# GpSimd multiplications that wait for a planned VectorE operation, three small copies on ScalarE, and a new order

## The chip, the cores and the metric

One core of a Trainium2 chip. Times are device microseconds of the whole program. The kernel before ran at a median of 355.24 us in three runs (353.91 to 357.82).

The program uses five engines of this core: TensorE (PE in the profile, its weight loads PEld), VectorE (DVE), ScalarE (ACT), GpSimd (POOL) and SyncE (SP, here an issuer of DMAs). The program gives each engine its instructions in a fixed order and ties the engines together with semaphores.

## The reference

```
q_p, k_p = phi(q), phi(k)              # phi(x): p = x @ w_phi ; p -= max|p| ; [exp(p), exp(-p)]
kv  = einsum('bhsf,bhsd->bhfd', k_p, v)
num = einsum('bhsf,bhfd->bhsd', q_p, kv)
den = einsum('bhsf,bhf->bhs', q_p, sum_s k_p) + 1e-6
x   = (num / den) as [batch, seq, heads*64]
x1, x2, x3 = split(x @ w_proj)         # 512 wide each
y   = x1 * irfft(rfft(x2) * rfft(filter)) * x3     # along seq, 576 long
out = y @ w_out
```

8 batches, 8 heads, 576 positions, 64 per head, 128 features. Inputs and output are fp32; the kernel works in bf16 with fp32 accumulation.

## The kernel before

The program is a list of 2467 nodes. A node is a few instructions of one engine; a fixed list ORDER gives the order in which nodes are emitted, and with it the order on each engine. A second list, SLOTS, gives each PSUM tile its bank. The work comes in 16 attention units (two per batch, nodes a0 to a15) and 8 batches of convolution and gate (m0 to m7).

Per unit, GpSimd does six multiplications: the values, scaled by exp(-max) or exp(max), for the key-value matmuls.

```python
def f_v(hp, sg):                       # nodes v00 v01 v10 v11: 128x512
    def f():
        v12 = c.v12[pair(hp) % 3]
        nc.gpsimd.tensor_tensor(
            out=v12[:, sg, :, 0:HD].rearrange("p (j c) d -> p j c d", j=2),
            in0=c.vs[b % 2][:, g, hp:hp + 3:2],
            in1=v12[:, sg, :, 64:65].rearrange(
                "p (j c) o -> p j c o", j=2).to_broadcast([P, 2, 4, HD]),
            op=ALU.mult)
    return f
# ... f_vt: the same for the last 64 rows, 128x260
```

VectorE folds the transposed attention output twice (f1 to f4), and copies some of it:

```python
def level2(sl, op):                    # nodes f3 f4: two SBUF inputs
    def f():
        eo = get_eo()
        TT(out=get_G()[0][:, k0:k0 + 2, sl, 0:145], in0=eo[:, :, :, 0:145],
           in1=eo[:, :, :, 288:143:-1], op=op)
    return f

def rem():                             # node fr, "the rest copy"
    G, Gr = get_G()
    nc.vector.tensor_copy(Gr[:, k0:k0 + 2, :, 0:17], G[:, k0:k0 + 2, :, 128:145])

def f_x0():                            # node x0, "the edge copies", before f1 and f2
    nc.vector.tensor_copy(xT()[:, kt0 + 1, 512:SEQ], xT()[:, kt0 + 1, SEQ:640])
    nc.vector.tensor_copy(xT()[:, kt0:kt0 + 2, SEQ:SEQ + 1],
                          xT()[:, kt0:kt0 + 2, 0:1])

def f_mx0():                           # node mx0: 128x20, fp32 to bf16, "the cast"
    nc.vector.tensor_copy(c.M2[i2][:, 0:20], mxq().rearrange("p c h -> p (c h)"))

def f_mtc():                           # node mt, from PSUM, "the transposed maxima"
    nc.vector.tensor_copy(c.mT[i2], c.open[n + "mtp"])
# ... cut: maxima, exponentials, products with the filter's spectrum (L1026), Y (L1032) and so on
```

Nodes that use the SBUF port that VectorE and GpSimd share are marked `lock=1`. In the kernel before the mark has no effect on the program. It is emitted like this:

```python
with tc.manual_schedule(engines={ET.PE, ET.Activation, ET.DVE, ET.Pool, ET.SP}):
    for i in ORDER:
        if nodes[i].fn is not None:
            nodes[i].fn()
```

## Time and profile before

| | before |
|---|---|
| median time | 355.24 us |
| span of the profiled run | 352.1 us |
| VectorE busy | 317.5 us (90%) |
| TensorE busy | 306.6 us (87%) |
| ScalarE / GpSimd busy | 270.1 / 163.1 us |
| chain that ended last | TensorE 45%, VectorE 43% |

The page of the kernel before: its span, the busy table (microseconds, share of the span, instructions), and the chain of work that ended last, followed back from the last instruction.

```profile
span 352.1 us, 8527 instructions
...
PE 306.6 (87%) x3253; PEld 202.3 (57%) x3253; DVE 317.5 (90%) x742; ACT 270.1 (77%) x664; POOL 163.1 (46%) x207
...
PE 45%; DVE 43%; DMA 6%; ACT 2%; issue 2%; DVEq 0%; ACTq 0%
```

Two engines look full, and the chain alternates between them. But a busy engine may be waiting inside an instruction. The timeline shows that (kernel before, in order of time; columns: start, duration, engine, line, operation, output<-inputs, count; in brackets the idle time before it and what ended it).

```profile
211.92 0.45 DVE L333 TENSOR_TENSOR eo_118<-xT_115 128x578 bf16<-128x578 bf16 x1
...
212.75 1.05 POOL L759 TENSOR_TENSOR v_104<-vs_73,v_104 128x512 bf16<-128x512 bf16 x1 [10.62 <-ACT v_104 L750]
...
212.91 0.92 DVE L980 COPY xT_115<-xT_115 128x2 bf16<-128x2 bf16 x1
...
213.77 0.90 POOL L799 TENSOR_TENSOR vt_107<-vt_135,emt_84 128x260 bf16<-128x260 bf16 x1
...
214.12 2.11 DVE L333 TENSOR_TENSOR eo_119<-xT_115 128x578 bf16<-128x578 bf16 x2
...
214.63 1.27 POOL L759 TENSOR_TENSOR v_106<-vs_73,v_106 128x512 bf16<-128x512 bf16 x1
...
215.87 1.28 POOL L759 TENSOR_TENSOR v_104<-vs_73,v_104 128x512 bf16<-128x512 bf16 x1
...
216.15 1.69 DVE L340 TENSOR_TENSOR G_681<-eo_118 128x580 bf16<-128x580 bf16 x2
```

A fold alone takes 0.45 us (first line). Beside multiplications two of them take 2.11 us, and a copy of two elements takes 0.92 us. VectorE and GpSimd go forward in lockstep.

From the trace I worked out one number, the **collision loss**: for each VectorE instruction, the time from the end of the one before it (or its own start, if later) to its own end, less the median of its line and shape; losses over 0.1 us are summed. It is 36.7 us here, of which 30 lie where the chain runs through VectorE. The losses in the first 16 us of the program, which meet no GpSimd multiplication, are in it too.

I also asked, for each stalled operation that could be placed in ORDER, whether the multiplication that it met comes earlier or later in ORDER. In 33 of 34 cases it comes later. GpSimd, busy only 46% of the time, runs ahead of its place in the plan.

### The profile page before, as it was taken

How to read it: one execution, taken by the hardware profiler on the slowest of the kernel's cores; microseconds unless marked ns; L12 is line 12 of the kernel's file. 1: busy time of each engine (PE TensorE's matmuls, PEld its weight loads, DVE VectorE, ACT ScalarE, POOL GpSimd, SP SyncE). 2: the span in 40 equal slices, each digit the busy share in tenths (PEclk: the TensorE clock that was granted, in tenths of full speed). 3: DMA queues.
4: the chain of work that ended last, by engine and by line, in shares of the span. 5: the costliest groups of instructions: out<-in, count | busy, mean ns of one | idle time of the engine just before them, and what ended most of it. 6: DMA issues, size and time to landing. Idle time of an engine off the chain costs nothing.

```text
span 352.1 us, 8527 instructions
## 1 busy us (share of the span) xinstructions
PE 306.6 (87%) x3253; PEld 202.3 (57%) x3253; DVE 317.5 (90%) x742; ACT 270.1 (77%) x664; POOL 163.1 (46%) x207
## 2 busy tenths in 40 slices
PE   1478796799989699899989998889998999999984
PEld 0346653368547385468736774469556864586441
DVE  8999998989989989999988999999999999998390
ACT  1698785389969388698979997878888997994633
POOL 8859764509635802485038904670457214330000
PEclk9987998999999899999999999999999999999999
DMA  7999999918976927449671995292792461001013
GB/s 98 137 164 173 158 154 178 179 36 80 187 200 83 128 48 188 127 52 153 136 195 16 135 187 179 56 129 40 140 186 52 55 165 61 0 2 62 2 60 149
DMA packets 97160, 39.87 MB, mean 113 GB/s; under 512 B 66080, under 2 KB 92000, under 8 KB 97120
## 3 DMA queue, kind: packets, MB, share of 16 engines
q0 software_dynamic: 40096, 16.85, 39.9%
q1 hardware_dynamic: 57024, 22.49, 29.4%
q8 instruction: 25, 0.41, 0.5%
q14 instruction: 15, 0.12, 0.1%
HBM read 33.75 MB, written 9.44 MB: 123 GB/s over the span
## 4 chain that ended last, share of the span: by engine, by line
PE 45%; DVE 43%; DMA 6%; ACT 2%; issue 2%; DVEq 0%; ACTq 0%
DVE mxk_82 L736 3%; DMA xT_115<-xn_113 3%; DMA xT_114<-xn_113 3%; DVE xn_113 L917 3%; DVE mxq_147 L675 3%; DVE G_681 L340 3%; DVE mxq_143 L675 2%; DVE Y L1032 2%; DVE P_973 L1026 2%; DVE P_974 L1026 2%; DVE eo_119 L333 2%; DVE ts L1091 2%; DVE mxk_83 L736 1%; DVE G_684 L340 1%; DVE eo_118 L333 1%
## 5 line engine op out<-in xcount | busy, mean ns | idle before, releaser
L1067 PEld LDWEIGHTS <-wproj 128*128 128x128 bf16 x512 | 33.8, 99 | 36.2 <-issue 13.5
L759 POOL TENSOR_TENSOR v_105<-vs_73,v_105 128x512 bf16<-128x512 bf16 x12 | 13.3, 1116 | 35.3 <-ACT emt_84 L792 16.5
L759 POOL TENSOR_TENSOR v_106<-vs_73,v_106 128x512 bf16<-128x512 bf16 x10 | 11.1, 1114 | 26.1 <-ACT v_106 L750 18.9
L1161 PEld LDWEIGHTS <-yT 128*128 128x128 bf16 x144 | 13.8, 98 | 15.2 <-DVE yT L1132 2.2
L1026 DVE TENSOR_TENSOR P_973<-CS,H_124 128x1024 bf16<-128x1024 bf16 (+1 forms) x24 | 17.3, 720 | 5.6 <-ACT CS L1021 5.5
L759 POOL TENSOR_TENSOR v_106<-vs_72,v_106 128x512 bf16<-128x512 bf16 x10 | 11.4, 1153 | 19.9 <-PE fi_2944 L1161 12.0
L759 POOL TENSOR_TENSOR v_104<-vs_73,v_104 128x512 bf16<-128x512 bf16 x10 | 11.6, 1171 | 19.5 <-ACT v_104 L750 19.5
L851 PEld LDWEIGHTS <-sel 128*128 128x128 bf16 x256 | 18.6, 100 | 2.9 <-issue 0.3
L759 POOL TENSOR_TENSOR v_104<-vs_72,v_104 128x512 bf16<-128x512 bf16 x12 | 13.3, 1108 | 10.2 <-ACT v_104 L750 10.1
L759 POOL TENSOR_TENSOR v_105<-vs_72,v_105 128x512 bf16<-128x512 bf16 x10 | 10.9, 1086 | 13.7 <-ACT v_105 L750 13.7
L1026 DVE TENSOR_TENSOR P_974<-CS,H_125 128x1024 bf16<-128x1024 bf16 (+1 forms) x24 | 17.0, 719 | 0.0
L842 PEld LDWEIGHTS <-wpp 128*128 128x128 bf16 x128 | 11.3, 99 | 7.1 <-issue 2.8
L1115 PEld LDWEIGHTS <-Y 128*128 128x128 bf16 x128 | 12.5, 98 | 2.9
L799 POOL TENSOR_TENSOR vt_107<-vt_131,emt_84 128x260 bf16<-128x260 bf16 x8 | 5.2, 661 | 15.2 <-ACT emt_84 L792 15.2
L517 POOL DMA_DIRECT2D qt<-in_q_dram x18 | 11.6, 647 | 0.4 <-DMA kt<-in_k_dram 0.4
L517 POOL DMA_DIRECT2D kt<-in_k_dram x18 | 11.6, 647 | 0.0
L1010 PEld LDWEIGHTS <-G_681 128*128 128x128 bf16 x64 | 6.1, 98 | 9.0 <-DVE G_681 L340 1.7
L1010 PEld LDWEIGHTS <-G_684 128*128 128x128 bf16 x64 | 6.1, 98 | 8.9 <-issue 2.7
L525 POOL DMA_DIRECT2D vt_135<-in_v_dram x16 | 10.2, 635 | 0.0
L525 POOL DMA_DIRECT2D vt_131<-in_v_dram x16 | 10.0, 635 | 0.2 <-issue 0.2
L669 PEld LDWEIGHTS <-qT_76 128*128 128x128 bf16 x64 | 6.1, 104 | 6.2 <-DVE qT_76 L632 3.5
L500 POOL DMA_DIRECT2D ks<-in_k_dram x9 | 8.3, 923 | 2.0 <-PE ttp L640 1.2
(2109 smaller groups left out, 1366.9 us busy)
## 6 DMA issues: line engine op xcount, KB each, us to landing
ks<-in_k_dram POOLq DMA_DIRECT2D x7, 512.0 KB, 7.7
qs<-in_q_dram POOLq DMA_DIRECT2D x7, 512.0 KB, 6.2
out_dram<-o_120 SPq DMA_DIRECT2D x12, 256.0 KB, 2.1
out_dram<-o_122 SPq DMA_DIRECT2D x12, 256.0 KB, 2.1
out_dram<-o_121 SPq DMA_DIRECT2D x12, 256.0 KB, 2.2
vs_73<-in_v_dram POOLq DMA_DIRECT2D x4, 512.0 KB, 6.1
wproj<-in_moe_w_proj_dram POOLq DMA_DIRECT2D x4, 384.0 KB, 7.5
vs_72<-in_v_dram POOLq DMA_DIRECT2D x3, 512.0 KB, 7.6
```

Source lines behind the costliest of these rows:

```text
L340: TT(out=get_G()[0][:, k0:k0 + 2, sl, 0:145], in0=eo[:, :, :, 0:145], in1=eo[:, :, :, 288:143:-1], op=op)
L517: nc.gpsimd.dma_start(out=dst()[64 * hp:64 * hp + 64, g0:g1].rearrange("p g j d -> p (g j) d"), in_=sv[hp, 512:SEQ, 2 * g0:2 * g1, :])
L525: nc.gpsimd.dma_start(out=c.vt[b % 2][64 * hp:64 * hp + 64, g, hp, :, 0:HD], in_=sv[hp, 512:SEQ, 2 * g:2 * g + 2, :])
L675: nc.vector.tensor_reduce(out=mxq()[:, 0:4, 2 * hp + j], in_=c.open[f"{n}qn{hp}{j}"], axis=AX.X, op=ALU.max, apply_absolute_value=True)
L736: nc.vector.tensor_reduce(out=c.mxk[i2][:, 8 * hp + 4 * j:8 * hp + 4 * j + 4], in_=c.open[f"{n}pk{hp}{j}"], axis=AX.X, op=ALU.max, apply_a ...
L759: nc.gpsimd.tensor_tensor(out=v12[:, sg, :, 0:HD].rearrange("p (j c) d -> p j c d", j=2), in0=c.vs[b % 2][:, g, hp:hp + 3:2], in1=v12[:, s ...
L851: nc.tensor.matmul(pp[:, ci, :], lhsT=c.sel[:, 4 * ci + 2 * hp + j, :], rhs=c.mT[i2], start=False, stop=True, skip_group_check=True)
L1010: nc.tensor.matmul(acc, lhsT=rem_block(c.G[b % 2], m, kt), rhs=c.wproj[:, kt, 512:1024], start=(kt == 0), stop=(kt == 3))
L1026: TT(out=p[:, sl, :], in0=c.CS[:, sl, :], in1=H[:, sl, :], op=ALU.mult)
L1067: nc.tensor.matmul(acc, lhsT=c.wproj[:, kt, base + m * P:base + (m + 1) * P], rhs=xT()[:, kt, s0:s1], start=(kt == 0), stop=(kt == 3))
L1115: nc.tensor.matmul(acc, lhsT=Y, rhs=c.IV[:, kt, 0:HALF], start=(i == 0), stop=(i == 2))
L1161: nc.tensor.matmul(acc, lhsT=c.yT[:, kt, ci * P:(ci + 1) * P], rhs=c.wout[:, kt, :], start=(kt == 0), stop=(kt == 3))
```

## The change

Its intent: let no multiplication start before the last port-using VectorE operation that the plan has ahead of it; take small copies from VectorE; and plan the order again with both in mind.

```diff
     def rem():
         G, Gr = get_G()
-        nc.vector.tensor_copy(Gr[:, k0:k0 + 2, :, 0:17], G[:, k0:k0 + 2, :, 128:145])
+        nc.scalar.copy(Gr[:, k0:k0 + 2, :, 0:17], G[:, k0:k0 + 2, :, 128:145])
...
-    c.add(n + "fr", "DVE", 113, [n + "f3", n + "f4"], rem, lock=1)
+    c.add(n + "fr", "ACT", act(136), [n + "f3", n + "f4"] + need_g, rem)
...
     def f_mtc():
-        nc.vector.tensor_copy(c.mT[i2], c.open[n + "mtp"])
+        nc.scalar.copy(c.mT[i2], c.open[n + "mtp"])
...
         def f_x0():
-            nc.vector.tensor_copy(xT()[:, kt0 + 1, 512:SEQ], xT()[:, kt0 + 1, SEQ:640])
-            nc.vector.tensor_copy(xT()[:, kt0:kt0 + 2, SEQ:SEQ + 1],
+            nc.scalar.copy(xT()[:, kt0 + 1, 512:SEQ], xT()[:, kt0 + 1, SEQ:640])
+            nc.scalar.copy(xT()[:, kt0:kt0 + 2, SEQ:SEQ + 1],
                                   xT()[:, kt0:kt0 + 2, 0:1])
... (functions of lock=1 nodes now return their last instruction; SLOTS and ORDER all new)
     with tc.manual_schedule(engines={ET.PE, ET.Activation, ET.DVE, ET.Pool, ET.SP}):
+        port = None
         for i in ORDER:
-            if nodes[i].fn is not None:
-                nodes[i].fn()
+            nd = nodes[i]
+            r = nd.fn() if nd.fn is not None else None
+            if nd.lock and r is not None:
+                if nd.eng == "DVE":
+                    port = r
+                elif port is not None:
+                    tc.add_manual_dep(r.ins, port.ins.name, mybir.DependencyInfo(
+                        mybir.DependencyClass.Sync, mybir.DependencyReason.DATA),
+                        reason="turns at the shared port")
```

Below, "the waits" (or gates) are the last part, "the copies" the first, "the order" the new ORDER and SLOTS.

## The prediction

> **What bounds the kernel now.** The profile's span is 352.1 us (354 us as timed in that run, median 355.24). The busy table has VectorE at 317.5 us (90%), TensorE 306.6 (87%), ScalarE 270.1 (77%), GpSimd 163.1 (46%). The chain that ended last is TensorE 45% and VectorE 43%, DMA 6%. So the two alternate as the limit, and neither is near the memory limit.
>
> VectorE's 317.5 us is not all work. Taking each instruction's time from the end of the one before, against the median of its shape, 56 instructions lose over 0.1 us each, 36.7 us together. In the groups view split by overlap with a GpSimd multiplication: the 128x580 fold takes 466 ns alone and 982 ns beside one, the 128x1024 product 694 against 1001, the 128x20 subtraction 168 against 816. Reductions and products that read PSUM do not change (681 against 683 ns). In the timeline at 212.9 to 217.8 us a 2-element copy, folds and their GpSimd partners end in lockstep. The Trainium skill's page "SBUF — State Buffer", section "Who interferes with whom", says that an op with two SBUF inputs, or a two-port copy, and a GpSimd op that reads SBUF exclude each other for the whole instruction; the trace agrees.
>
> Of the stalled operations that I could place in the planned order, 33 of 34 met a GpSimd multiplication that the plan puts *later*: GpSimd ran ahead of its turn. About 30 of the 36.7 us lies on the chain.
>
> **What changes.**
> 1. Each GpSimd multiplication (64 of 1.06 us, 32 of 0.62 us at the median) must wait for the last port-using VectorE operation before it in the plan. That forbids the early meetings, nearly all there are. It does not forbid late ones, and the 128x20 cast (four stalls, 2.3 us in all) is still not counted as a port user.
> 2. Per unit, the rest copy (0.13 us), the transposed-maxima copy (0.13) and the edge copies (0.09 + 0.17) leave VectorE: about 9 us of uncontended work, 4 us of it on the chain. ScalarE gains about 10 us (estimate from its 128x8 and 128x260 operations, 0.13 and 0.27 us), and its queue now sits in the fold's path.
> 3. The whole order and the PSUM slots are replanned. The gaps left for GpSimd between port users grow: 2.8 us of planned non-port VectorE work on average before, 4.8 after; none is shorter than the multiplication in it, eight were.
>
> **Sum.** VectorE falls to about 275 us (317.5 - 36.7 - 9, plus some 3 to 6 for late meetings). Removing all 34 us on the chain would give 318 us, but TensorE needs 290 us at the median of each shape, starts slowly (37 us busy in the first 60) and ends with about 5 idle. At 318 it would have to run without a gap in between; at some 96% there I get about 328 us of span. ScalarE, near 282 us, is the next limit.
>
> Predicted: 331 us, 319 to 345 in 8 of 10. Faster by over 2%: 0.92; within 2%: 0.07; slower: 0.01.
>
> **What would show it.** VectorE busy 270 to 285 us; folds and products beside GpSimd near their times alone; collision loss below 10 us; GpSimd waits now ended by VectorE; ScalarE 278 to 290; TensorE share above 90%, and most of the chain.
>
> **What would make it wrong.** Gated GpSimd operations finish late and meet the next port user anyway; they delay the key-value matmuls or the loads queued behind them; the copies queue up on ScalarE and hold the folds; or the new order has gaps of its own on TensorE.

## The result, and the profile after

The changed kernel is correct and runs at a median of 335.92 us (335.79 to 337.65, four runs) against 356.04 us (four runs). The ratio is 0.9448, 95% interval 0.9385 to 0.9512. Ratios here are the mean time of one kernel's fast runs over that of the other's fast runs of the same rounds, so not quite the ratio of the medians: the kernel before scatters by some 2.7% (350.2 to 359.9 us over all its runs). In the rounds of this result all four of its runs count as fast (mean 356.0 us). In the rounds of the experiments below a faster run was among them, so those above some 355.5 us count as slow and are left out; the fast ones have a mean of 353.3 to 353.6 us. Differences against the kernel before are therefore given below from fast runs of the same rounds.

| | before | after |
|---|---|---|
| span | 352.1 us | 334.2 us |
| VectorE busy | 317.5 us | 279.1 us |
| collision loss on VectorE | 36.7 us | 3.9 us |
| ScalarE busy | 270.1 us | 279.3 us |
| TensorE busy | 306.6 us (87%) | 300.3 us (90%) |
| chain | TensorE 45%, VectorE 43% | TensorE 71%, VectorE 9% |

The page of the changed kernel, the same three parts.

```profile
span 334.2 us, 8513 instructions
...
PE 300.3 (90%) x3220; PEld 201.6 (60%) x3253; DVE 279.1 (84%) x678; ACT 279.3 (84%) x728; POOL 156.7 (47%) x207
...
PE 71%; DVE 9%; DMA 9%; ACT 6%; issue 2%; POOL 1%; DVEq 0%; ACTq 0%
```

The chain has left VectorE. The timeline of the changed kernel, with a unit's folds and the multiplications after them. The multiplication at 205.92 had to wait for the subtraction that ended at 205.75:

```profile
174.60 0.62 POOL L801 TENSOR_TENSOR vt_107<-vt_141,emt_84 128x260 bf16<-128x260 bf16 x1 [0.44 <-ACT emt_84 L794]
...
174.87 0.38 DVE L706 CAST M_1_132<-mxq_134 128x20 bf16<-128x20 f32 x1
...
203.15 0.46 DVE L342 TENSOR_TENSOR G_618<-eo_118 128x580 bf16<-128x580 bf16 x1
...
203.52 0.46 DVE L342 TENSOR_TENSOR G_618<-eo_119 128x580 bf16<-128x580 bf16 x1
...
205.35 0.18 DVE L706 CAST M_0_128<-mxq_130 128x20 bf16<-128x20 f32 x1
...
205.57 0.18 DVE L709 TENSOR_TENSOR M_0_128<-mxq_130,M_0_128 128x20 bf16<-128x20 f32 x1
...
205.92 1.06 POOL L761 TENSOR_TENSOR v_104<-vs_73,v_104 128x512 bf16<-128x512 bf16 x1 [4.13 <-ACT Gr_619 L348]
...
207.09 0.68 DVE L1092 TENSOR_TENSOR ts<-x_3651,x1s 128x512 bf16<-128x512 f32 x1
...
207.78 0.69 DVE L738 TENSOR_REDUCE mxk_83<-pk_3575 128x4 f32<-128x512 f32 x1
```

GpSimd sits out the folds and multiplies beside operations that read PSUM; each runs at its time alone. The first two lines are what is left: the cast, 0.18 us alone, takes 0.38 because the plan does not count it as a port user. Seven of its 16 executions are stalled, 3.4 of the 3.9 us.

Busy time by stretch tells where the time came from. Kernel before (columns: stretch in us, its length, busy time of each engine with instruction counts, granted TensorE clock, DMA share, GB/s):

```profile
0.00:60.00 60.00, 37.09 (x387) 26.53 (x388) 56.39 (x165) 43.20 (x109) 43.42 (x66) 0.93 1.16 151
60.00:300.00 240.00, 223.49 (x2410) 147.76 (x2409) 225.12 (x487) 195.69 (x489) 114.13 (x137) 0.99 0.71 118
```

The changed kernel, order of columns as above (PE, PEld, DVE, ACT, POOL):

```profile
0.00:60.00 60.00, 38.45 (x424) 28.55 (x427) 53.08 (x163) 44.99 (x121) 42.24 (x65) 0.89 1.17 152
60.00:300.00 240.00, 233.78 (x2605) 158.54 (x2632) 207.06 (x468) 218.55 (x577) 114.48 (x143) 0.99 0.73 118
```

The start is as slow as before (38 of 60 us on TensorE). The steady part gained: TensorE is busy 97% of it instead of 93%, and does more matmuls in it (2605 records against 2410).

### The profile page after: what moved, and what is told of

It reads as the page before. It is cut to its first block, busy times and chain, and to the rows that moved or that the text cites. A ratio compares the mean times of both kernels' runs of the same rounds, so it can differ in the third digit from the quotient of the medians.

```text
span 334.2 us, 8513 instructions
## 1 busy us (share of the span) xinstructions
PE 300.3 (90%) x3220; PEld 201.6 (60%) x3253; DVE 279.1 (84%) x678; ACT 279.3 (84%) x728; POOL 156.7 (47%) x207
## 4 chain that ended last, share of the span: by engine, by line
PE 71%; DVE 9%; DMA 9%; ACT 6%; issue 2%; POOL 1%; DVEq 0%; ACTq 0%
DMA qt<-in_q_dram 4%; DMA xT_114<-xn_112 2%; DMA xT_115<-xn_113 2%; DMA out_dram<-o_120 1%; ACT Ekm_92 L745 1%; DVE r L277 1%; ACT Ekp_89 L745 1%; DMA out_dram<-o_122 1%; PE tk L685 1%; PE tq L814 1%; PE tq L809 1%; DVE SD_981 L1124 1%; PE x_2964 L1068 1%; ACT o_120 L1167 0%; DVE SD_981 L1128 0%
## 5 line engine op out<-in xcount | busy, mean ns | idle before, releaser
L761 POOL TENSOR_TENSOR v_104<-vs_73,v_104 128x512 bf16<-128x512 bf16 x10 | 10.5, 1056 | 23.1 <-ACT o_121 L1167 11.4
L761 POOL TENSOR_TENSOR v_106<-vs_73,v_106 128x512 bf16<-128x512 bf16 x10 | 10.5, 1057 | 21.9 <-DVE G_618 L342 14.8
L1027 DVE TENSOR_TENSOR P_974<-CS,H_124 128x1024 bf16<-128x1024 bf16 (+1 forms) x24 | 14.1, 596 | 7.7 <-ACT CS L1022 7.7
L761 POOL TENSOR_TENSOR v_104<-vs_72,v_104 128x512 bf16<-128x512 bf16 x12 | 12.6, 1057 | 16.3 <-DVE G_621 L342 7.5
L761 POOL TENSOR_TENSOR v_106<-vs_72,v_106 128x512 bf16<-128x512 bf16 x10 | 10.5, 1056 | 14.6 <-DVE M_0_128 L706 14.4
L761 POOL TENSOR_TENSOR v_105<-vs_73,v_105 128x512 bf16<-128x512 bf16 x12 | 12.7, 1062 | 7.9 <-ACT Eqp_96 L859 7.8
L761 POOL TENSOR_TENSOR v_105<-vs_72,v_105 128x512 bf16<-128x512 bf16 x10 | 10.5, 1062 | 11.6 <-DVE rc_86 L913 7.5
L1027 DVE TENSOR_TENSOR P_975<-CS,H_125 128x1024 bf16<-128x1024 bf16 (+1 forms) x24 | 14.1, 597 | 2.0 <-ACT CS L1022 1.9
L801 POOL TENSOR_TENSOR vt_107<-vt_141,emt_84 128x260 bf16<-128x260 bf16 x8 | 4.9, 619 | 14.6 <-DVE M_0_128 L706 9.8
L626 PE MATMUL qtp<-ident,qs 128*128 128x128 bf16 x16 | 2.1, 312 | 10.6 <-DMA qs<-in_q_dram 10.6
L1011 PEld LDWEIGHTS <-G_621 128*128 128x128 bf16 x64 | 6.2, 98 | 7.1 <-issue 0.3
L1011 PEld LDWEIGHTS <-G_618 128*128 128x128 bf16 x64 | 6.2, 98 | 6.4
L801 POOL TENSOR_TENSOR vt_107<-vt_145,emt_84 128x260 bf16<-128x260 bf16 x8 | 4.9, 616 | 9.7 <-ACT emt_84 L794 8.1
```

Source lines behind the costliest of these rows:

```text
L761: return nc.gpsimd.tensor_tensor(out=v12[:, sg, :, 0:HD].rearrange("p (j c) d -> p j c d", j=2), in0=c.vs[b % 2][:, g, hp:hp + 3:2], in1=v ...
L801: return nc.gpsimd.tensor_tensor(out=c.vt12[i2][:, sg], in0=c.vt[b % 2][:, g], in1=c.emt[i2][:, sg:sg + 1].to_broadcast([P, 2, 2, 65]), op ...
L1011: nc.tensor.matmul(acc, lhsT=rem_block(c.G[b % 2], m, kt), rhs=c.wproj[:, kt, 512:1024], start=(kt == 0), stop=(kt == 3))
L1027: return TT(out=p[:, sl, :], in0=c.CS[:, sl, :], in1=H[:, sl, :], op=ALU.mult)
```

## Experiments

The first theory was that of the prediction: early meetings at the port are the loss, and the waits remove them. The rival: the new order does it, since it leaves wider gaps. A third part, the copies, had to be told apart from both. So I made all combinations of the three (the order "old" or "new"; the kernel before and the changed kernel are two of the eight), three rounds each beside the kernel before. All eight are correct.

**w_old: the waits alone.** The kernel before with the changed emission loop; instruction order on each engine is the same as before.

```diff
+            if nd.lock and r is not None:
+                if nd.eng == "DVE":
+                    port = r
+                elif port is not None:
+                    tc.add_manual_dep(r.ins, port.ins.name, ...)
```

> The kernel before, with nothing changed but the waits of the GpSimd multiplications (old order, copies still on VectorE). If the early meetings at the shared port are the cause and the waits by themselves remove them, VectorE's collision loss falls from 36.7 us to below 10 and the time to 345 us or less. If the replanned order is the cause, the old order's gaps are too narrow for gated multiplications: the loss stays above 15 us as late meetings, or GpSimd's lateness holds TensorE, and the time stays at 350 us or more.

Measured: 420.18 us, ratio 1.190 (1.178 to 1.203). This is the second expectation in kind (350 us or more, late meetings, TensorE held up); that it would cost 67 us (420.2 against 353.3 for the kernel before, fast runs) neither foresaw. The collision loss did fall, to 18.7 us, and all 17 stalls that could be placed are now *late* meetings (the multiplication comes earlier in ORDER than the operation that it met). And GpSimd is on the chain. The chain of this run, by engine, from its page:

```profile
PE 49%; POOL 18%; DVE 12%; DMA 7%; ACT 7%; issue 5%; POOLq 0%; DVEq 0%; ACTq 0%
```

The waits view of this run (the engine, tile and line that waited <- what ended the wait: us in total, times, longest us):

```profile
PE kv L886 <- POOL v L761: 50.0, 17, 9.3
ACT KVs L896 <- PE kv L890: 38.5, 13, 9.3
```

The key-value matmuls wait 50 us for multiplications. In the kernel before, the multiplications that ran ahead of their places were what fed those matmuls in time. The old order, read as a timetable, has them too late: by the kernel's own planned durations, the TensorE work listed between a multiplication's place and the matmul that needs it is 2.2 us at the median, while the six of a unit take 5.5 us (4 x 1.06 + 2 x 0.62). In the new order it is 3.6 us at the median.

**c_old: the copies alone.** The old order, no waits.

```diff
-    c.add(n + "fr", "DVE", 113, ..., rem, lock=1)       # and mt, x0 alike
+    c.add(n + "fr", "ACT", act(136), ..., rem)
```

> The kernel before, with only the small copies moved to ScalarE (old order, no waits). Meetings theory: at most the 4 us that the copies and the stalls of the copies themselves have on the chain, so 346 to 356 us, with a collision loss still above 25 us. If the work taken off VectorE were the cause, 342 us or less.

Measured: 373.98 us, ratio 1.058 (1.044 to 1.071): slower by more than the interval, which neither expectation allowed. The collision loss is 29.1 us. The busy table and the chain of its page:

```profile
PE 312.6 (83%) x3217; PEld 205.0 (55%) x3253; DVE 304.3 (81%) x678; ACT 281.8 (75%) x728; POOL 162.2 (43%) x207
...
PE 44%; DVE 29%; ACT 15%; DMA 8%; issue 3%; DVEq 0%; ACTq 0%
```

A line of its waits view:

```profile
DVE eo L335 <- ACT xT L981: 12.6, 7, 3.4
```

VectorE has less work and is less busy, and the program is longer. The folds now wait for edge copies that stand in ScalarE's queue at the place that ORDER gave them when they were VectorE's. ScalarE's part of the chain rose from 2% to 15%. Work was taken off a full engine and a wait put in its place. This is read from the profile; no run singles out one of the three copies.

**wc_old: waits and copies, old order.**

> The kernel before with waits and copies both changed, in the old order. Meetings theory: 336 to 345 us, since only the order differs from the changed kernel. Replan theory: 348 us or more.

Measured: 437.97 us, ratio 1.240 (1.224 to 1.257), again the replan side of the expectation. The two harms nearly add up: 67 and 20 us by themselves, 84 together.

**c_new: the changed kernel without the waits.**

```diff
-            if nd.lock and r is not None:
+            if False and nd.lock and r is not None:
```

> The changed kernel without the waits (new order, copies on ScalarE). Meetings theory: GpSimd runs ahead again, VectorE's collision loss is 15 us or more, and the time is 344 to 356 us. Replan theory: the wider gaps do the work, the loss stays below 10 us, and the time is 334 to 340 us.

Measured: 344.04 us, ratio 0.976 (0.964 to 0.989). The early meetings are back: collision loss 23.6 us, 29 of 32 placed stalls early. So wide gaps in the plan do not keep the two engines apart; the waits do. The chain of its page:

```profile
PE 42%; DVE 31%; ACT 14%; DMA 8%; issue 3%; POOL 1%; DVEq 0%; ACTq 0%; POOLq 0%
```

VectorE is back on the chain with 31%. In the new order the waits are worth 8.1 us (344.0 - 335.9), though they take 20 us off VectorE's loss.

**new_only: the new order alone**, copies on VectorE, no waits.

> The new order and PSUM slots alone: no waits, the copies back on VectorE. If the new order is itself most of the gain: 342 us or less. If it is worth little without waits and copies: 348 us or more, with a collision loss of 25 us or more. Between: it shares the gain.

Measured: 363.74 us, ratio 1.032 (1.023 to 1.040), collision loss 25.7 us. Alone, the new order is a loss.

**w_new: the new order with the waits**, copies on VectorE.

> The new order with the waits, the copies back on VectorE. If the move of the copies matters little in an order that has room: 336 to 340 us, VectorE busy about 288 us. If ScalarE was the right place for them in this order: 341 us or more.

Measured: 347.76 us, ratio 0.986 (0.978 to 0.993), VectorE busy 286.5 us, collision loss 4.5 us. Here the waits are worth 16 us (363.7 - 347.8), and the copies another 12 (347.8 - 335.9), three times the 4 us that they had on the old chain.

The eight together (medians; collision loss from each profile):

| order | waits | copies on | median us | ratio | collision loss us |
|---|---|---|---|---|---|
| old | no | VectorE | 356.0 (the kernel before) | 1 | 36.7 |
| old | yes | VectorE | 420.2 | 1.190 | 18.7 |
| old | no | ScalarE | 374.0 | 1.058 | 29.1 |
| old | yes | ScalarE | 438.0 | 1.240 | 18.9 |
| new | no | VectorE | 363.7 | 1.032 | 25.7 |
| new | yes | VectorE | 347.8 | 0.986 | 4.5 |
| new | no | ScalarE | 344.0 | 0.976 | 23.6 |
| new | yes | ScalarE | 335.9 (the changed kernel) | 0.945 | 3.9 |

No single part is a gain by itself. From the kernel before, the waits cost 67 us, the copies 20 and the order 10. With the new order, either of the other two gives a small gain (ratios 0.976 and 0.986), and both together the whole of it.

So both first theories fell in their plain form. The new one: collisions are the loss, but a gate removes it only if the order gives each multiplication a turn early enough. That needs the price of the collisions by itself, without gates. I took away what makes them collide, the reading.

**nc_old: no collisions, no gates, old order** (wrong result). A fill writes where the multiplication wrote, after the same ScalarE operations and loads.

```diff
-            nc.gpsimd.tensor_tensor(out=v12[...], in0=c.vs[...], in1=v12[..., 64:65]..., op=ALU.mult)
+            return nc.gpsimd.memset(v12[...], 1.0)
...
+                    tc.add_manual_dep(r.ins, d.ins.name, ..., reason="as the multiplication did")
```

> Wrong result on purpose. The kernel before in its old order, without waits, with each GpSimd multiplication replaced by a fill of the same destination that waits for the same ScalarE operations and loads but reads nothing. Expected to take about as long on GpSimd (1.0 and 0.55 us, estimated from the 128-element fill of 0.31 us and the one-element fill of 0.10). If a GpSimd operation that reads nothing leaves VectorE's two-input operations alone, the collision loss falls below 8 us. Then the time says what the collisions cost in the old order: 320 to 332 us if the chain's 30 us was right, 345 us or more if the VectorE loss was mostly hidden behind TensorE.

Measured: 331.28 us, ratio 0.937 (0.924 to 0.949); collision loss 4.4 us. But a fill took only 0.53 and 0.31 us, half of what it replaces, so two things had changed.

**nc_new: the same in the new order**, copies on ScalarE, no waits.

> Wrong result on purpose. The changed kernel without its waits, with the same fills in place of the multiplications. Against the changed kernel (336 us) it shows what the gates themselves cost: 335 to 338 us if they cost nothing, 330 us or less if holding GpSimd back delays something. Against the run without waits (344 us) it shows what the collisions cost in the new order: 7 us or more if the waits are worth what they remove.

Measured: 334.08 us, ratio 0.948 (0.939 to 0.956), with the same flaw.

**nc2_old: two fills for each multiplication**, 1.05 and 0.63 us, so that GpSimd is as long as before (155.2 us busy against 163.1 with its stalls).

> Wrong result on purpose. As the run with fills in the old order, but with two fills for each multiplication, since one took only half as long (0.53 and 0.31 us against 1.06 and 0.62). If the collisions were what cost the time in the old order, it stays at 327 to 335 us. If half of that gain came from a GpSimd that was done sooner, it rises to 340 us or more.

Measured: 332.56 us, ratio 0.941 (0.929 to 0.953), collision loss 3.9 us. The busy table and the chain of its page:

```profile
PE 301.6 (91%) x3217; PEld 202.3 (61%) x3253; DVE 285.8 (86%) x742; ACT 269.5 (81%) x664; POOL 155.2 (47%) x303
...
PE 72%; DVE 15%; ACT 6%; DMA 4%; issue 2%; DVEq 0%; ACTq 0%
```

On GpSimd little but the reading was taken away, in the old order, with the copies on VectorE and GpSimd free to run ahead, and the profile looks like that of the changed kernel: chain on TensorE with 72%, VectorE at 286 us. Collisions cost the kernel before about 21 us (353.4 - 332.6, fast runs of the same rounds). That is its whole distance to the changed kernel, 17 us by this count and 20 by the medians of the first rounds. The fills also change the numbers that TensorE multiplies, but its granted clock was the same (0.979 in this profile, 0.980 in that of the kernel before).

**nc2_new: two fills, new order.**

> Wrong result on purpose. Two fills for each multiplication, in the new order, without the waits. 333 to 337 us if only collisions matter; then the waits of the changed kernel (336 us) remove nearly all that collisions cost there, and holding GpSimd back costs at most 3 us. 340 us or more if GpSimd's own length is on the chain.

Measured: 337.68 us, just above the expected 333 to 337, ratio 0.957 (0.948 to 0.966), collision loss 0.9 us. It is no faster than the changed kernel (335.92), which has gates and real multiplications. So the gates recover all that collisions cost in the new order, and cost nothing that can be seen (the two were timed in different rounds, and half a per cent between them means nothing). Nor is the new order better as such: without collisions and gates, the old one (copies on VectorE) is at 332.6 us and the new one (copies on ScalarE, as it was planned) at 337.7.

**mx0: the cast counted as a port user**, in the changed kernel, to remove the stalls that are left.

```diff
-        nc.vector.tensor_copy(c.M2[i2][:, 0:20], mxq()...)
+        return nc.vector.tensor_copy(c.M2[i2][:, 0:20], mxq()...)
...
-      + unit("mtp"), f_mx0)
+      + unit("mtp"), f_mx0, lock=1)
```

> The changed kernel with the 128x20 cast counted as a port user too, so that no GpSimd multiplication planned after it starts before it. It has the 3.4 us of stalls that are left, but only 0.5 us of them on the chain. Collision loss on VectorE below 1.5 us, time within 1% of the changed kernel, 334 to 338 us. If the residual stalls mattered: 333 us or less.

Measured over five rounds: 346.97 us (345.25 to 348.91), ratio 0.983 (0.974 to 0.992), 11 us slower than the changed kernel, where 334 to 338 us and a loss below 1.5 us were expected. The collision loss rose to 10.7 us. All 14 stalls that could be placed are late meetings; the largest losses are on the products of line 1027. The chain of its page:

```profile
PE 64%; DVE 10%; ACT 9%; DMA 8%; POOL 5%; issue 3%; DVEq 0%; ACTq 0%; POOLq 0%
```

A line of its waits view:

```profile
PE kv L886 <- POOL v L761: 6.7, 3, 3.8
```

GpSimd has 5% of the chain, up from 1%, and key-value matmuls wait for it. It is the waits-alone run in small: a gate that the order was not planned for holds a group of multiplications until after its gap, and they meet the next port users. Removing 3.4 us of stalls, 0.5 of them on the chain, cost 11 us. So the changed kernel stands as the best correct version that I ran.

**port_probe: which operations collide** (a kernel of its own, wrong result). VectorE runs each kind alone, then beside eight GpSimd multiplications, then beside eight number fills (IOTA) that write but read nothing.

> Wrong result on purpose: a probe of its own. VectorE runs six kinds of operation in a row, alone, then beside eight GpSimd multiplications of 128x512, then beside eight GpSimd number fills that read nothing. The port theory: the 128x580 fold and the 128x20 subtraction (two inputs in SBUF) take one GpSimd operation each, about 1.06 us, beside the multiplications, and their time alone beside the fills; the reduction and the product that read PSUM change in neither; the cast and the copy within SBUF wait in both, as two-port operations. Rival, that everything on VectorE slows with GpSimd busy: the PSUM operations get longer too.

Timeline of the probe (a row merges several instructions: its count is at the end):

```profile
4.41 1.93 DVE L38 TENSOR_TENSOR fo<-fa,fb 128x580 bf16<-128x580 bf16 x4
...
11.50 1.81 DVE L47 COPY cb<-ca 128x136 bf16<-128x136 bf16 x8
...
39.80 5.13 POOL L58 TENSOR_TENSOR vo<-va,vb 128x512 bf16<-128x512 bf16 x4
39.88 0.16 DVE L72 COPY dn<-gm 128x1 bf16<-128x1 bf16 x1 [4.83 <-POOL gm L71]
39.95 5.29 DVE L38 TENSOR_TENSOR fo<-fa,fb 128x580 bf16<-128x580 bf16 x4
...
122.84 1.80 POOL L61 IOTA vi<- 128x512 int32 x3
122.93 0.16 DVE L72 COPY dn<-gm 128x1 bf16<-128x1 bf16 x1 [2.56 <-POOL gm L71]
123.00 1.94 DVE L38 TENSOR_TENSOR fo<-fa,fb 128x580 bf16<-128x580 bf16 x4
...
151.86 2.42 POOL L61 IOTA vi<- 128x512 int32 x4
151.95 0.16 DVE L72 COPY dn<-gm 128x1 bf16<-128x1 bf16 x1 [0.29 <-POOL gm L71]
152.02 2.31 DVE L47 COPY cb<-ca 128x136 bf16<-128x136 bf16 x4
```

Four folds take 1.93 us alone, 5.29 beside multiplications, and 1.94 beside fills that read nothing. Four copies take 2.31 us beside those same fills (eight take 1.81 alone). Steady duration of one operation, from its start to its end, in the trace:

| VectorE operation | alone | beside multiplications | beside number fills |
|---|---|---|---|
| fold, two SBUF inputs, 128x580 | 0.46 us | 1.29 | 0.46 |
| subtraction, two SBUF inputs, 128x20 | 0.18 | 1.01 and 0.18 in turn | 0.18 |
| cast within SBUF, 128x20 | 0.18 | 1.00 and 0.18 in turn | 0.59 |
| copy within SBUF, 128x136 | 0.20 | 1.20 | 0.59 |
| reduction from PSUM, 128x512 | 0.69 | 0.69 | 0.69 |
| product of PSUM and SBUF, 128x512 | 0.69 | 0.69 | 0.69 |

The port theory holds in every row, but for one detail: it expected each subtraction and cast to wait for a multiplication, and only every second one does. The rival is refuted by the last two rows. This is what the Trainium skill's page "SBUF — State Buffer", section "Who interferes with whom", states: two SBUF inputs contend with a GpSimd operation that reads, a two-port copy with any, and an operation with at most one SBUF input, outside the two-port modes, not at all. It is also why fills could stand in for multiplications above: only the small copies still met them.

## Why the prediction was right

- *VectorE loses 36.7 us to collisions, nearly all early, and about 30 are on the chain.* Right in kind. With the reading taken away and GpSimd just as long, the old order runs at 332.6 us, 21 us faster. So 30 us on the chain were worth 21, since TensorE, at 302 us busy, took over, as the prediction's sum had it.
- *The waits forbid early meetings.* Shown: 23.6 us of loss without them, 3.9 with them, in the same order. *They do not forbid late ones, and the cast is not counted.* Right: seven of the ten stalls that remain are the cast's.
- *The copies have 4 us on the chain.* Wrong as a value of the move. In the old order it costs 20 us; in the new one, with the waits, it gains 12. The busy time moved as estimated (ScalarE +9.2 us; the 18 rest copies last 0.33 us each but overlap with their neighbours and add 0.20 each).
- *The sum.* VectorE 279.1 us (said: 275, shown as 270 to 285), loss 3.9 (below 10), ScalarE 279.3 (278 to 290), chain on TensorE with 71%. TensorE's share is 89.9%, said to be above 90. The time is 335.9, 5 us above the 331 predicted and in the range. The term that was mis-sized is TensorE's own work: I took 290 us, the median of each shape, and it stayed busy for 300.3. The rest was near: 97.4% busy between 60 and 300 us (233.78 of 240), said to be 96%. Redoing the sum with 300 gives (300 - 38 - 7) / 0.974 + 72 = 334 us, the measured span; that is bookkeeping with the run's own numbers, not a test. By stretch, with the medians of the run's own shapes, about half of the excess lies in the first 60 us: 38.6 us busy there against 28.2 at the medians (kernel before: 37.5 and 25.9). The prediction took the busy 37 off a total counted at medians, and so left some 11 us too few for the rest. Why the matmuls of the start take longer is not shown.
- *GpSimd's waits now ended by VectorE.* Right, though the waits view does not show it, since it names whichever operation ended last before the start (for the second longest wait, the cast, which gates nothing). With each multiplication's gate taken from ORDER, 28 multiplications come after an idle time of over 0.15 us, 126.8 us in all; 19 of them, 108.1 us, start 0.09 to 0.23 us after the end of their gate. None of the 96 starts before its gate has ended.
- *What it did not say.* It gave the waits and the copies a value each, as if they could be added to any order, and named the replanning only as wider gaps. The runs show the opposite: waits and copies are harmful in the old order. The full gain belongs to the three together. That the total still came out near 331 us is in part luck: it rests on TensorE as the floor, which hid that the values given to the parts were wrong. "Gated operations finish late", in the list of what would make it wrong, is just what happens when the waits are applied without the new order.

Still open: why the new order alone is 10 us slower than the old one. It was planned for copies on ScalarE; with the copies there and no waits it is at 344 us, which fits, but no run singles out a cause. ORDER and SLOTS were always exchanged together, so what each is worth is not known. The scatter of the kernel before (350 to 360 us) is not explained either.

## What to carry to other kernels

When VectorE is busy but its operations vary in length, look for a GpSimd operation beside the long ones: the waiting is inside the instruction, and no view of waits shows it. Here a semaphore kept the two apart at no visible cost, but only where the order gave the gated work a turn well before its consumer; gating, or moving a copy to another engine's queue, without planning the order again cost 3 to 24% here. To price such a collision before planning around it, replace the one operation by another of the same length that reads nothing.

## What the Trainium skill lacked or had wrong

- "SBUF — State Buffer", section "Who interferes with whom": right on who contends (the probe's table), but of the time it says only that the second one to issue blocks for the whole instruction. With both queues full they alternate: one 128x580 fold for each multiplication, a fold then lasting 1.29 us against 0.46 alone; and of the 128x20 subtractions and casts two go through for each multiplication (1.01 and 0.18 us). The multiplications on GpSimd show 1.25 us beside folds, 1.15 without.
- "SBUF — State Buffer", section "Summary: rules for kernel authors": it advises to schedule whichever is off the critical path. It does not say that keeping GpSimd back is itself dangerous: waits in an order not made for them cost 67 us (353 to 420), and one more gate in an order made for the others 11 us (336 to 347).
- "GPSIMD Engine Reference", section "Common operations": no time for a fill. A bf16 fill of 128x512 took 0.53 us and of 128x260 0.31, half the multiplication of the same size (1.06 and 0.62); my estimate from a smaller fill was 1.0.
- "VectorE: DVE Perf Modes", section "The TRN2 errata": its row for ScalarE gives 0.30 us for a 136-element copy within SBUF (224 + 136 cycles at 1.2 GHz, an estimate from that page); the records of the 18 rest copies show 0.33.
